# A long convolution woven into a feed-forward kernel: one pool for the kernel factors of all channel groups, earlier spectra, stores on another queue, another hand-out

## The chip, the cores and the metric

The kernel runs on one core of one Trainium2 chip. The time is what the device reports for one execution, in microseconds. The core has a matrix engine (PE, with its weight loads shown apart as PEld), a vector engine (DVE), a scalar engine (ACT), a general engine (POOL) and a sync engine (SP). SP, POOL and ACT can each start transfers between the chip's memory and the core; the profile names a started transfer by the queue of its engine (SPq, POOLq).

## The reference

The layer has two halves. A long causal convolution comes first, and a feed-forward part with ReLU after it; both are modulated by six vectors made from the condition c.

```
mod = silu(c) @ w_mod                      # sa, ca, ga, sb, cb, gb
h   = layernorm(x) * (1 + ca) + sa
K   = 2 * Re( sum_n C[d,n] * exp(A[d,n]*dt[d]*l) )     # l = 0..2047
x   = x + ga * ( causal_conv(h, K) + D_skip * h )      # by FFT in the reference
h   = layernorm(x) * (1 + cb) + sb
x   = x + gb * ( relu(h @ w1) @ w2 )
```

x is 2048 tokens by D = 576 channels, N = 128 states, w1 is 576 x 4608 and w2 is 4608 x 576, all in float32.

## The kernel before

**Tiling.** The 2048 tokens are cut into four blocks of 512. The convolution is done block by block in a transformed domain: the kernel K of each of four distances and the input of each block are transformed (function `transform` and the butterflies), their products are summed over the blocks (`product`), and the sum is transformed back and added to x (`inverse`). The transformed tiles, called spectra, hold 128 x 2304 numbers, 1152 KB each; they are stored in the chip's memory (Ud, Kd, Rd) and fetched again by POOL's queue (`load`).

**The kernel K** is not read but computed: for 12 channel groups of 48 channels each, `KGen.first` builds three factors, W1, W2 and Z, in the first 235 us and stores them (W1d, W2d, Zd). For distance 0 it multiplies them at once. For distances 1, 2 and 3 the function `KGen.rest` does it later: DVE turns W1 by Z once for each distance (`rot`, lines 459 to 465, four instructions), PE multiplies the result with W2 (`products`, line 490: 192 small matmuls per channel group, each with 16 columns per distance), ACT moves the products into a tile called ker (line 500), and after six channel groups `store` (line 431) writes ker to memory as kd, two transfers for each distance. `conv` reads it back as kt.

**The feed-forward part** runs through the four blocks, and in each through 36 groups g of 128 hidden units. To keep float32 accuracy each factor is split into a high and a low part and three products are made. `first(g)` has 14 matmuls into hps (line 1273); ACT makes the high part hh by ReLU (line 1278), DVE the low part hl (line 1279); `second(g)` has 14 matmuls of hh and hl with w2, into five accumulators (line 1299). PE's order is first(g+1), then second(g). In block 0 the weights come as float32 tiles r (SP, lines 1230 and 1234) and are split by ACT (1246, 1256) and DVE (1249, 1259, 1260); the low parts are stored (L1d, L2d) and read back in the later blocks, where DVE has no splits to do.

**What sets the order.** The convolution of block s+1 is a generator that is woven into the feed-forward part of block s. `step(g)` runs four times per group and takes pieces from the generator until a budget is reached: `rate` is the work handed out per step, a piece of DVE work counts its estimated microseconds, a burst of matmuls counts 0.7, `room` bounds the DVE work of the last four steps, and a piece that yields -1 ends the step. At the end of a block what is left of the generator is taken all at once. In block 0 the generator does `rest` for channel groups 0 to 5 and all three distances, then `rest` for 6 to 11 and distance 1 alone, each from a pool of its own, then conv(1). Block 1 adds block 0's result to x and writes it out (`finish(0)`), does `rest` for 6 to 11 and distances 2 and 3, then conv(2). Block 2 does finish(1) and conv(3). Within the limits of its program a scheduler moves instructions on each engine, so an instruction may stand earlier than the generator asked for.

**Buffers around the change.** In `rest`, W0 (the loaded W1), Z and W2 have two buffers each and are loaded together, one channel group ahead; W1r, the turned factor, has two; ker has one. The spectra share six buffers, and the products' half tiles T two. The x tile of block 1 comes from the pool `xb`, which is opened after `rest`. conv(1)'s normalised tile h2 has four buffers of its own, the tile xf two.

Of the kernel before, what the change touches and what calls it, by code (L numbers as in the profile page):

```python
# [49 lines left out]
class KGen:  # L50
# [384 lines left out]
    def rest(self, psum, hs, blocks):  # L435

# [3 lines left out]
        na = 16 * len(blocks)  # L440
        with ExitStack() as ctx:
            pt = k.pool(ctx, f"kr{hs[0]}{blocks[0]}", side="right")

            def load(h):
                W2 = pt.tile([P, 2, 32, H], F32, tag="W2", bufs=2, name=f"W2r_{h}")
                W0 = pt.tile([P, 16, 2, H], F32, tag="W0", bufs=2, name=f"W0_{h}")
                Z = pt.tile([P, 2, 2, H], F32, tag="Z", bufs=2, name=f"Zr_{h}")
                d = nc.gpsimd.dma_start
                d(out=W0.rearrange("p a r c -> p (a r c)"), in_=k.W1d[h])
                d(out=Z.rearrange("p i r c -> p (i r c)"), in_=k.Zd[h])  # L450
                d(out=W2.rearrange("p r b c -> p (r b c)"), in_=k.W2d[h])
                return W2, W0, Z

# [13 lines left out]

            def rots(W1, W0, Z):
# [12 lines left out]
            def products(h, W1, W2):  # L481
                if h % 6 == 0:
                    ke[0] = pt.tile([P, na, 72], F32, tag="ke", bufs=1, name=f"ker_{h}")
# [20 lines left out]
                if h % 6 == 5:  # L504
                    yield -1
                    for i, s in enumerate(blocks):
                        self.store(
                            s, h // 6, ke[0][:, 16 * i : 16 * i + 16].rearrange("p a q -> p (a q)"),
                            nc.gpsimd,
                        )  # L510

            nxt = load(hs[0])
# [21 lines left out]
class Body:  # L534
# [198 lines left out]
    def main(self, ctx, kg, hooks):  # L733
# [10 lines left out]
        def block0():  # L744
            yield from kg.rest(self.cps, range(0, 6), (1, 2, 3))
            yield from kg.rest(self.cps, range(6, 12), (1,))
            self.xp.append(self.pool(ctx, "xb"))
            self.x2p.append(self.xp[1])
            pool(1)
            yield from self.conv(1)  # L750

        def block1():
            yield from self.finish(0)
            yield -1
            self.cvs.close()
            yield from kg.rest(self.cps, range(6, 12), (2, 3))
            pool(2)
            yield from self.conv(2)
# [6 lines left out]
        with ExitStack() as c:  # L765
# [4 lines left out]
            self.nps = 4  # L770
# [13 lines left out]
        self.nps = 1  # L784
# [116 lines left out]
    def conv(self, s):  # L901
# [25 lines left out]
        yield -1  # L927
# [44 lines left out]
        def product(p, Y):  # L972
            def pair(t):
                Ka = Ks[p] if t == 0 else self.load(self.Kd[s - t][p], "Ka")
                Ua = Us[p] if (t == s and Us[p] is not None) else self.load(self.Ud[t][p], "Ua")
                return Ka, Ua
# [3 lines left out]
            yield -1  # L980
# [53 lines left out]
        Us, Ks, Vs = [], [], []  # L1034
# [20 lines left out]
        else:  # L1055
# [6 lines left out]
            ZK = self.spec("Z")  # L1062
            yield from both(spec_U(1, Z1), mm_K(1, ZK))
# [13 lines left out]
        else:  # L1077
            yield from both(spec_K(1, ZK), after(3, inverse(0, Vs[0])))
# [3 lines left out]
        yield -1  # L1082
        yield -1
# [15 lines left out]
        h2 = [self.cvl.tile([P, D + 64], F32, tag="h2", bufs=4, name="h2") for _ in range(4)]  # L1099
# [7 lines left out]
        for kk in (4, 0, 1, 2, 3):  # L1107
# [3 lines left out]
            xf = self.cvl.tile([P, 512], F32, tag="xf", bufs=2, name="xf")  # L1111
# [109 lines left out]
    def ffn(self, gens):  # L1221
# [87 lines left out]
        def step(g):  # L1309
# [5 lines left out]
            room = (9.0, 7.0, 7.0, 7.0)[g // NF] - sum(recent[-3:])  # L1315
            recent.append(0.0)
            while done[0] < target and v < min(room, 2.7) and pe < 2:
                w = next(gen, 0)
                if gen.gi_frame is None or w == -1:
                    return  # L1320
                if w is None:
                    pe += 1
                    done[0] += 0.7
                else:
                    v += w
                    recent[-1] = v
                    done[0] += w
# [85 lines left out]
    def rate(self, b):  # L1413
        return (2.12, 1.8, 1.4, 0.5)[b]
# [82 lines left out]
```

## Time and profile before

| what | value |
|---|---|
| median of 3 runs | 1408.16 us (1401.38 to 1409.32) |
| the profiled execution | 1404.99 us; its span, first to last instruction, 1403.2 us |
| mean granted PE clock | 0.936 of full speed |
| busy in the span | PE 1258.5, DVE 889.9, ACT 497.4, POOL 179.2 us |
| moved | 348.21 MB, 247 GB/s over the span |

The profile's page gives busy time per engine, the chain of work that ended last, and the costliest groups of instructions by line of the code. A view by windows gives each engine's busy time, the granted PE clock and the share of time that the transfer engines were busy, for a stretch of the span. A timeline gives single rows: start, duration, engine, line, operation, tile written and tiles read, and in brackets the idle time ahead with what ended it.

Marks for block 0: the first low part hl of group 0 starts at 237.71 us, that of group 13 at 354.73, 18 at 390.13, 23 at 461.58, 28 at 514.28, 35 at 591.01, the first two groups of block 1 at 616.27 and 618.34, and the next at 631.87. The four blocks thus take some 380 us from the first mark to the seventh, and then 771.33 us from 631.87 to the end.

### The profile page before, as it was taken

What the parts mean: (1) busy time and instruction counts of PE and PEld (TensorE: products, weight loads), DVE (VectorE), ACT (ScalarE), POOL (GpSimd) and SP (SyncE); (2) the same over time, 40 slices, a digit from 0 to 9 for tenths busy, and PEclk for the clock granted to TensorE, in tenths of its full rate; (3) what the DMA queues carried; (4) which work ended last, traced back from release to release, by engine and by line L of the source; (5) the groups of instructions that cost most, each with busy time, mean ns of one, the idle gap of its engine ahead of it and who ended that gap; (6) DMA issues with size and microseconds to landing.
All of it is one profiled execution on the core that took longest, in us unless ns stands there. A gap on an engine that the chain in (4) does not pass through costs nothing.

```text
span 1403.2 us, 26027 instructions
## 1 busy us (share of the span) xinstructions
PE 1258.5 (90%) x10720; PEld 994.5 (71%) x10720; DVE 889.9 (63%) x1324; ACT 497.4 (35%) x863; POOL 179.2 (13%) x277
## 2 busy tenths in 40 slices
PE   4565677899988997789999999999999999999997
PEld 2354555678866775567777787777887878888886
DVE  5989967999565778749825779563899332010102
ACT  4778323222211430252224322633332353232321
POOL 0677520000110100011010110000000000000000
PEclk9667786999999998889999999999999999999999
DMA  8658875767796776649777988584989657666661
GB/s 258 244 210 306 319 242 188 243 223 248 285 366 244 266 253 229 240 175 399 277 243 259 332 301 321 160 279 147 396 307 342 195 160 222 197 197 198 198 189 68
DMA packets 120843, 348.21 MB, mean 248 GB/s; under 512 B 23948, under 2 KB 24244, under 8 KB 109716
## 3 DMA queue, kind: packets, MB, share of 16 engines
q1 hardware_dynamic: 102260, 222.09, 47.4%
q0 software_dynamic: 17952, 123.08, 23.2%
q8 instruction: 84, 1.38, 0.4%
q10 hardware_dynamic: 512, 1.38, 0.3%
q14 instruction: 35, 0.29, 0.1%
HBM read 262.73 MB, written 83.76 MB: 247 GB/s over the span
## 4 chain that ended last, share of the span: by engine, by line
PE 62%; DVE 20%; DMA 9%; issue 4%; ACT 2%; POOL 1%; SPq 0%; ACTq 0%; POOLq 0%; DVEq 0%
PE acc L1299 24%; PE hps L1273 24%; PE kps L490 5%; PE ps_f L815 4%; DMA r<-in_w_dram 3%; DMA Ua<-Ud 3%; DVE T L998 3%; DVE Y L1000 3%; PE kps L71 2%; PE ph L71 2%; DMA Ud<-U 1%; DMA Zr<-Zd 1%; DVE hl L1279 1%; DVE Y L994 1%; DVE T L62 1%
## 5 line engine op out<-in xcount | busy, mean ns | idle before, releaser
L1273 PE MATMUL hps<-xh,w 128*128 128x512 f32 x1152 | 395.9, 403 | 0.7 <-issue 0.7
L1299 PE MATMUL acc<-w,hh 128*128 128x512 f32 x1152 | 368.2, 402 | 2.8 <-ACT hh L1278 2.8
L1279 DVE SCALAR_TENSOR_TENSOR hl<-hps,hh 128x512 fp32r<-128x512 f32 x144 | 99.2, 689 | 328.4 <-ACT hh L1278 328.1
L1299 PEld LDWEIGHTS acc<-w,hh 128*128 128x128 f32 x1152 | 217.0, 190 | 50.7 <-ACT hh L1278 3.6
L1273 PEld LDWEIGHTS hps<-xh,w 128*128 128x128 f32 x1152 | 219.0, 191 | 47.3
L1299 PE MATMUL acc<-w,hl 128*128 128x512 f32 x576 | 227.3, 406 | 20.4 <-DVE hl L1279 20.3
L1273 PE MATMUL hps<-xl,w 128*128 128x512 f32 x576 | 230.5, 401 | 0.9 <-DVE xl L47 0.9
L1278 ACT ACTIVATE hh<-hps 128x512 fp32r<-128x512 f32 x144 | 86.0, 597 | 317.9 <-PE hps L1273 317.9
L1256 ACT ACTIVATE w<-r 128x576 fp32r<-128x576 f32 x144 | 98.8, 686 | 279.8 <-PE acc L1299 226.0
L1299 PEld LDWEIGHTS acc<-w,hl 128*128 128x128 f32 x576 | 109.1, 191 | 48.3 <-DVE hl L1279 25.3
L1273 PEld LDWEIGHTS hps<-xl,w 128*128 128x128 f32 x576 | 110.0, 191 | 26.9 <-DVE xl L47 2.3
L1246 ACT ACTIVATE w<-r 128x640 fp32r<-128x640 f32 x144 | 105.4, 732 | 44.6 <-DMA r<-in_w_dram 44.2
L1273 PE MATMUL hps<-xs,w 128*128 128x512 f32 x288 | 100.9, 421 | 2.0 <-DVE xs L47 1.8
L490 PEld LDWEIGHTS kps<-W1r,W2r 128*32 128x32 f32 x3456 | 67.5, 146 | 35.6 <-issue 24.6
L490 PE MATMUL kps<-W1r,W2r 128*32 128x48 f32 (+2 forms) x3456 | 76.9, 238 | 11.9 <-issue 7.5
L71 PE MATMUL kps<-W,W 128*32 128x16 f32 x2304 | 44.8, 217 | 40.1 <-POOL W L68 29.0
L1000 DVE TENSOR_TENSOR Y<-Y,T 128x1152 f32<-128x1152 f32 x60 | 79.4, 1350 | 0.0
L71 PEld LDWEIGHTS kps<-W,W 128*32 128x32 f32 x2304 | 40.3, 150 | 51.1 <-POOL W L68 30.9
L816 ACT ACTIVATE Z<-ps_f 128x288 f32<-128x288 f32 x120 | 49.0, 409 | 70.7 <-PE ps_f L815 69.2
L1411 POOL DMA_DIRECT2D out_dram<-x x16 | 8.7, 546 | 458.3 <-DVE x L1403 455.9
L1273 PEld LDWEIGHTS hps<-xs,w 128*128 128x128 f32 x288 | 55.7, 196 | 15.1 <-ACT xh L47 2.1
L1299 PE MATMUL acc<-hh,w 128*128 128x512 f32 x144 | 57.9, 402 | 1.0 <-DVE w L1259 1.0
(234 smaller groups left out, 1593.5 us busy)
## 6 DMA issues: line engine op xcount, KB each, us to landing
r<-in_w_dram SPq DMA_DIRECT2D x144, 320.0 KB, 4.5
r<-in_w_dram SPq DMA_DIRECT2D x144, 288.0 KB, 3.2
w<-L1d SPq DMA_DIRECT2D x108, 320.0 KB, 2.7
w<-L2d SPq DMA_DIRECT2D x108, 288.0 KB
W2r<-W2d POOLq DMA_DIRECT2D x18, 1536.0 KB, 9.1
W2d<-W SPq DMA_DIRECT2D x12, 1536.0 KB, 8.6
Ua<-Ud POOLq DMA_DIRECT2D x15, 1152.0 KB, 9.6
W<-W1d POOLq DMA_DIRECT2D x18, 768.0 KB, 9.8
```

Source lines behind the costliest of these rows:

```text
L71: self.tc.keep_in_program_order(self.nc.tensor.matmul(*args, **kw))
L490: nc.tensor.matmul(ps[32 * dd : 32 * dd + 32, q, :], W2[:, r, :, ch], W1[:, :, r, ch], start=(r == 0), stop=(r == 1),)
L815: nc.tensor.matmul(o, fc[:, n2, c, :], src(n2), start=True, stop=True)
L816: ev = nc.scalar.activation(Z[:, n2, c], ps[:, :PC], AF.Copy)
L998: v(T, k, u, op=ALU.mult)
L1000: v(y, y, T, op=op or ALU.add)
L1246: nc.scalar.activation(w[:, 0], r, AF.Copy)
L1256: nc.scalar.activation(w[:, 0:D], r, AF.Copy)
L1273: nc.tensor.matmul(ps, a, x, start=(i == 0), stop=(i == 13))
L1278: nc.scalar.activation(hh, ps, AF.Relu)
L1279: nc.vector.scalar_tensor_tensor(hl, ps, 0.0, hh, op0=ALU.max, op1=ALU.subtract)
L1299: nc.tensor.matmul(acc[i], a, x, start=(f == 0 and seen[i] == 1), stop=(f == NF - 1 and seen[i] == (3 if i < 4 else 2)),)
```

## The change

- `rest` is called once for block 0. A plan says which distances each channel group takes: 0 to 5 all three, 6 to 11 the first. W0 and Z have three buffers and are loaded two channel groups ahead; W2 keeps two buffers and is loaded one ahead. Three one-distance groups share one tile W1r of 48 columns. ker has the full width throughout and one buffer.
- The kd stores are started by SP and no longer by POOL.
- The x tile of block 1 gets a pool of its own, opened before `rest`.
- Spectra have seven buffers instead of six, T three instead of two (in the first convolution still six and two). conv(1) to conv(3) take h2 and xf out of the spectra's buffers, xf four of them.
- The first input spectrum of each product is asked for before the butterflies that precede the product.
- The places that ended a step (`yield -1`) ahead of the transforms, ahead of each product and after the last `back` are gone for conv(1) to conv(3).
- In block 0 a burst of matmuls counts 0.35 instead of 0.7, room is 7.5 instead of 9.0, the rate 2.15 instead of 2.12.

```diff
-    def rest(self, psum, hs, blocks):
+    def rest(self, psum, plan):
         ...
-            def load(h):
-                W2 = pt.tile([P, 2, 32, H], F32, tag="W2", bufs=2, name=f"W2r_{h}")
-                W0 = pt.tile([P, 16, 2, H], F32, tag="W0", bufs=2, name=f"W0_{h}")
-                Z = pt.tile([P, 2, 2, H], F32, tag="Z", bufs=2, name=f"Zr_{h}")
+            def load0(h):
+                W0 = pt.tile([P, 16, 2, H], F32, tag="W0", bufs=3, name=f"W0_{h}")
+                Z = pt.tile([P, 2, 2, H], F32, tag="Z", bufs=3, name=f"Zr_{h}")
                 d(out=W0.rearrange("p a r c -> p (a r c)"), in_=k.W1d[h])
                 d(out=Z.rearrange("p i r c -> p (i r c)"), in_=k.Zd[h])
+                return W0, Z
+
+            def load2(h):
+                W2 = pt.tile([P, 2, 32, H], F32, tag="W2", bufs=2, name=f"W2r_{h}")
                 d(out=W2.rearrange("p r b c -> p (r b c)"), in_=k.W2d[h])
-                return W2, W0, Z
+                return W2
         ...
-                    ke[0] = pt.tile([P, na, 72], F32, tag="ke", bufs=1, name=f"ker_{h}")
+                    ke[0] = pt.tile([P, most, 72], F32, tag="ke", bufs=1, name=f"ker_{h}")[:, :na]
         ...
                         self.store(
                             s, h // 6, ke[0][:, 16 * i : 16 * i + 16].rearrange("p a q -> p (a q)"),
-                            nc.gpsimd,
+                            nc.sync,
                         )
         ...
+            nxt = [load0(hs[0])]
+            W2 = load2(hs[0])
+            nxt.append(load0(hs[1]))
             yield -1
             prev = iter(())
-            for h in hs:
-                W2, W0, Z = nxt
-                W1 = pt.tile([P, na, 2, H], F32, tag="W1", bufs=2, name=f"W1r_{h}")
-                yield from spread(rots(W1, W0, Z), prev, len(blocks))
-                if h + 1 in hs:
-                    nxt = load(h + 1)
+            for i, h in enumerate(hs):
+                W0, Z = nxt.pop(0)
+                if i + 2 < len(hs):
+                    nxt.append(load0(hs[i + 2]))
+                na = 16 * len(plan[h])
+                if used + na > most:
+                    all1 = pt.tile([P, most, 2, H], F32, tag="W1", bufs=2, name=f"W1r_{h}")
+                    used = 0
+                W1 = all1[:, used : used + na]
+                used += na
+                yield from spread(rots(h, W1, W0, Z), prev, len(plan[h]))
                 prev = products(h, W1, W2)
+                if i + 1 < len(hs):
+                    W2 = load2(hs[i + 1])
             yield from prev
         ...
         def block0():
-            yield from kg.rest(self.cps, range(0, 6), (1, 2, 3))
-            yield from kg.rest(self.cps, range(6, 12), (1,))
+            self.x2p.append(self.pool(ctx, "x2b"))
+            yield from kg.rest(
+                self.cps, {h: (1, 2, 3) if h < 6 else (1,) for h in range(NH)}
+            )
             self.xp.append(self.pool(ctx, "xb"))
-            self.x2p.append(self.xp[1])
         ...
-        return self.cv.tile([P, 4, 2, PC], F32, tag="S", bufs=6, name=name)
+        return self.cv.tile([P, 4, 2, PC], F32, tag="S", bufs=self.ns, name=name)
         ...
-        return self.cvl.tile([P, 4, PC], F32, tag="T", bufs=2, name=name)
+        return self.cvl.tile([P, 4, PC], F32, tag="T", bufs=self.ns - 4, name=name)
         ...
-                Ua = Us[p] if (t == s and Us[p] is not None) else self.load(self.Ud[t][p], "Ua")
+                Ua = first.pop(p) if p in first else Us[p] if (t == s and Us[p] is not None) else self.load(self.Ud[t][p], "Ua")
         ...
-            yield -1
+            if not s:
+                yield -1
         ...
             ZK = self.spec("Z")
+            first[0] = self.load(self.Ud[0][0], "Ua")
             yield from both(spec_U(1, Z1), mm_K(1, ZK))
         ...
         yield from back(1, Y)
-        yield -1
-        yield -1
         ...
-            room = (9.0, 7.0, 7.0, 7.0)[g // NF] - sum(recent[-3:])
+            room = (7.5, 7.0, 7.0, 7.0)[g // NF] - sum(recent[-3:])
         ...
-                    done[0] += 0.7
+                    done[0] += (0.35, 0.7, 0.7, 0.7)[g // NF]
         ...
-        return (2.12, 1.8, 1.4, 0.5)[b]
+        return (2.15, 1.8, 1.4, 0.5)[b]
```

The new lines push the later code down by some 20 lines: line 1279 (hl) before is line 1300 after, 1299 (acc) is 1320, 500 (ker) is 507.

Three places show what the change does to the order of the instructions. The rows give line, operation, tile written and tiles read with their numbers, and the shape.

**DVE at the end of block 0.** x_1 is the x tile of block 1, x_0 that of block 0; oT and t are block 0's result on its way into x_0 (`finish(0)`); xs and xl are the low parts of conv(1)'s result, which the first matmuls of block 1 read. Before, the last low part hl of block 0 is followed by 28 instructions until the two first hl of block 1; the last of these rows:

```order
L863 BN_STATS st_6298<-x_1_5282 128x6
L872 BN_AGGR mv<-st_6296 128x2
L872 BN_AGGR mv<-st_6297 128x2
L872 BN_AGGR mv<-st_6298 128x2
L1407 TENSOR_TENSOR oT<-oT,m_gb 128x512
L876 RECIPROCAL mv<-mv 128x1 x3
L877 SCALAR_TENSOR_TENSOR mv<-mv 128x1 x3
L1409 TENSOR_TENSOR x_0_280<-x_0_280,oT 128x512
L1407 TENSOR_TENSOR oT<-oT,m_gb 128x512 x2
L1409 TENSOR_TENSOR x_0_280<-x_0_280,oT 128x512 x2
L1119 TENSOR_TENSOR xs_6264<-xf,xs_6264 64x512
L1121 TENSOR_TENSOR xl_6263<-xf,xh_6262 128x512 x4
```

After, the last hl of block 0 is the second hl row here:

```order
L1280 TENSOR_TENSOR w_6352<-r_6231,w_6352 128x64
L1281 TENSOR_TENSOR w_6352<-r_6231,w_6352 128x512
L1300 SCALAR_TENSOR_TENSOR hl<-hps,hh 128x512
L1140 TENSOR_TENSOR xs_6148<-xf,xs_6148 64x512
L1300 SCALAR_TENSOR_TENSOR hl<-hps,hh 128x512
L1142 TENSOR_TENSOR xl_6147<-xf,xh_6146 128x512 x4
L1300 SCALAR_TENSOR_TENSOR hl<-hps,hh 128x512
L1428 TENSOR_TENSOR oT<-oT,m_gb 128x512
L1430 TENSOR_TENSOR x_0_280<-x_0_280,oT 128x512
L1428 TENSOR_TENSOR oT<-oT,m_gb 128x512
L1422 TENSOR_TENSOR t_6472<-ps_o_6467,m_gb 128x256
L1430 TENSOR_TENSOR x_0_280<-x_0_280,oT 128x512
```

The statistics of x_1 and conv(1)'s last inverse stand several groups earlier, the low parts xs and xl stand around block 0's last hl, and block 0's result comes after the first hl of block 1.

**ACT where ker passes from the first six channel groups to the last six.** ker with 48 columns is that of groups 0 to 5, ker with 16 columns that of 6 to 11; w is a split weight, r the loaded one. Before:

```order
L500 ACTIVATE ker_3101<-kps 128x48x6
L1278 ACTIVATE hh<-hps 128x512
L1246 ACTIVATE w_4475<-r_4443 128x640
L1256 ACTIVATE w_4678<-r_4445 128x576
L1278 ACTIVATE hh<-hps 128x512
L1246 ACTIVATE w_4684<-r_4627 128x640
L1256 ACTIVATE w_4845<-r_4629 128x576
L1278 ACTIVATE hh<-hps 128x512
L1246 ACTIVATE w_4851<-r_4785 128x640
L1256 ACTIVATE w_5003<-r_4787 128x576
L1278 ACTIVATE hh<-hps 128x512
```

After:

```order
L1277 ACTIVATE w_4514<-r_4267 128x576
L1267 ACTIVATE w_4322<-r_4265 128x640
L507 ACTIVATE ker_3119<-kps 128x48x6
L1299 ACTIVATE hh<-hps 128x512 x2
L507 ACTIVATE ker_4337<-kps 128x16x6
L1267 ACTIVATE w_4520<-r_4455 128x640
L507 ACTIVATE ker_4337<-kps 128x16x6
L1277 ACTIVATE w_4698<-r_4457 128x576
L507 ACTIVATE ker_4337<-kps 128x16x6
L1267 ACTIVATE w_4704<-r_4647 128x640
L507 ACTIVATE ker_4337<-kps 128x16x6
L1277 ACTIVATE w_4877<-r_4649 128x576
```

Before, four groups' hh lie between the last wide ker and the first narrow one (two more rows of w stand ahead of it); after, one group's pair of hh does, and the narrow ones follow each other with one w between.

**SP at the same place.** r is a loaded weight tile, L1d and L2d the stored low parts, kd the stored products. Before, with the kd stores on POOL:

```order
L1350 DMA L1d_141<-w_3994 128x640
L1234 DMA r_4316<-in_w_dram 128x576
L1230 DMA r_4314<-in_w_dram 128x640
L1350 DMA L2d_177<-w_4168 128x576
L1350 DMA L1d_142<-w_4071 128x640
```

After:

```order
L1371 DMA L1d_141<-w_4036 128x640
L431 DMA kd_0_59<-ker_3119 64x1152 x2
L431 DMA kd_0_61<-ker_3119 64x1152 x2
L431 DMA kd_0_63<-ker_3119 64x1152 x2
L1251 DMA r_4455<-in_w_dram 128x640
L1255 DMA r_4457<-in_w_dram 128x576
L1371 DMA L2d_177<-w_4316 128x576
```

The six stores stand in SP's order ahead of the next two weight loads. By the same listings the last turn of the factors (`rot`) stands in group 17 of block 0, before it stood in group 22; five and a half channel groups of products stand in groups 16 to 18, about two in each (before 1.2 in each of the groups 18 to 22); and the forward transforms of conv(1) stand in groups 20 to 24 (before 25 to 28). On DVE the eight statistics of the unchanged x_1 stand in the first 235 us, among the last instructions of conv(0); on POOL the load of x_1 stands after the copy of the condition (line 701 before), ahead of all of `rest`.

More of the change, by code (lines that the diff above doesn't have):

```diff
@@ L433, in store @@
             )
-    def rest(self, psum, hs, blocks):
+    def rest(self, psum, plan):
         nc, k = self.nc, self.k
         v = nc.vector.tensor_tensor
-        na = 16 * len(blocks)
+        hs = list(plan)
         with ExitStack() as ctx:
-            pt = k.pool(ctx, f"kr{hs[0]}{blocks[0]}", side="right")
-            def load(h):
-                W2 = pt.tile([P, 2, 32, H], F32, tag="W2", bufs=2, name=f"W2r_{h}")
-                W0 = pt.tile([P, 16, 2, H], F32, tag="W0", bufs=2, name=f"W0_{h}")
-                Z = pt.tile([P, 2, 2, H], F32, tag="Z", bufs=2, name=f"Zr_{h}")
-                d = nc.gpsimd.dma_start
+            pt = k.pool(ctx, f"kr{len(hs)}", side="right")
+            most = used = 16 * max(len(b) for b in plan.values())
+            d = nc.gpsimd.dma_start
+            def load0(h):
+                W0 = pt.tile([P, 16, 2, H], F32, tag="W0", bufs=3, name=f"W0_{h}")
+                Z = pt.tile([P, 2, 2, H], F32, tag="Z", bufs=3, name=f"Zr_{h}")
                 d(out=W0.rearrange("p a r c -> p (a r c)"), in_=k.W1d[h])
                 d(out=Z.rearrange("p i r c -> p (i r c)"), in_=k.Zd[h])
+                return W0, Z
+            def load2(h):
+                W2 = pt.tile([P, 2, 32, H], F32, tag="W2", bufs=2, name=f"W2r_{h}")
                 d(out=W2.rearrange("p r b c -> p (r b c)"), in_=k.W2d[h])
-                return W2, W0, Z
+                return W2
             def rot(out, X, Z, i):
@@ L466, in rot, with rots @@
                 yield 0.95
-            def rots(W1, W0, Z):
+            def rots(h, W1, W0, Z):
+                blocks = plan[h]
                 a = [W1[:, 16 * i : 16 * i + 16] for i in range(len(blocks))]
@@ L481, in products @@
             def products(h, W1, W2):
+                blocks = plan[h]
+                na = 16 * len(blocks)
                 if h % 6 == 0:
-                    ke[0] = pt.tile([P, na, 72], F32, tag="ke", bufs=1, name=f"ker_{h}")
+                    ke[0] = pt.tile([P, most, 72], F32, tag="ke", bufs=1, name=f"ker_{h}")[:, :na]
                 for half in range(2):
@@ L755, in block1 @@
             self.cvs.close()
-            yield from kg.rest(self.cps, range(6, 12), (2, 3))
+            yield from kg.rest(self.cps, {h: (2, 3) for h in range(6, NH)})
             pool(2)
@@ L769, in main @@
             self.cvl = self.pool(c, "cvl", side="right")
-            self.nps = 4
+            self.nps, self.ns = 4, 6
             mods, ffn = self.mod_late(), self.ffn(gens)
@@ L783, in main @@
             self.vec = nc.vector
-        self.nps = 1
+        self.nps, self.ns = 1, 7
         self.cps = self.pool(ctx, "cps", space=PSUM)
@@ L1032, in back @@
             Vs.append(V)
-        Us, Ks, Vs = [], [], []
+        Us, Ks, Vs, first = [], [], [], {}
         ZU = self.spec("Z") if s == 0 else None
@@ L1077, in conv @@
         else:
+            first[1] = self.load(self.Ud[0][1], "Ua")
             yield from both(spec_K(1, ZK), after(3, inverse(0, Vs[0])))
@@ L1081, in conv @@
         yield from back(1, Y)
-        yield -1
-        yield -1
         xh = xp.tile([P, 4, 512], F32R, tag="xh", bufs=1, name=f"xh_{s}")
@@ L1098, in conv @@
         yield 2.0
-        h2 = [self.cvl.tile([P, D + 64], F32, tag="h2", bufs=4, name="h2") for _ in range(4)]
+        flat = lambda name: self.spec(name).rearrange("p a b c -> p (a b c)")
+        h2 = [flat("h2")[:, : 2 * (D + 64)].rearrange("p (n d) -> p n d", n=2) for _ in range(2)]
+        h2 = [h2[n2 // 2][:, n2 % 2] for n2 in range(4)]
+        xfs = [flat("xf")[:, : 4 * 512].rearrange("p (k t) -> p k t", k=4)]
+        xfs = [xfs[0][:, k] for k in range(4)]
         for n2 in range(4):
@@ L1110, in conv @@
                 nc.tensor.transpose(ps[:, n2], h2[n2][:, kk * P : (kk + 1) * P], self.ident)
-            xf = self.cvl.tile([P, 512], F32, tag="xf", bufs=2, name="xf")
+            xf = xfs[kk % 4]
             ps = ps.rearrange("p a b -> p (a b)")
```

1 line of the change is left out of this document (removed).

## The prediction

> **What bounds the kernel now.** I read the page's busy times first, then the windows cut at the marks of block 0, then the idle times on PE's timeline, and last the chain of waits for what lies behind them.
>
> ```profile
> PE 1258.5 (90%) x10720; PEld 994.5 (71%) x10720; DVE 889.9 (63%) x1324; ACT 497.4 (35%) x863; POOL 179.2 (13%) x277
> ```
>
> PE is busy 90% of the span, so a gain must come from the stages where it is not, or runs at a lower clock. The windows (time, then busy time of PE, PEld, DVE, ACT, POOL, then granted PE clock, transfer share, GB/s):
>
> ```profile
> 237.71:354.73 117.02, 113.27 (x1321) 89.23 (x1320) 114.52 (x117) 28.15 (x48) 7.58 (x15) 0.97 0.72 249
> 354.73:390.13 35.40, 35.40 (x325) 28.99 (x325) 16.98 (x27) 10.29 (x17) 7.43 (x14) 1.00 0.83 304
> 390.13:461.58 71.45, 60.73 (x1294) 47.93 (x1293) 42.55 (x56) 12.65 (x28) 7.72 (x14) 0.93 0.81 296
> 461.58:514.28 52.70, 52.70 (x219) 38.38 (x218) 39.46 (x71) 23.59 (x53) 5.29 (x9) 1.00 0.81 287
> 514.28:591.01 76.73, 58.81 (x221) 44.99 (x220) 66.58 (x88) 13.68 (x22) 3.18 (x6) 0.88 0.62 227
> 591.01:618.34 27.33, 20.95 (x81) 15.10 (x82) 15.56 (x41) 17.45 (x32) 2.20 (x5) 0.77 0.20 64
> 631.87:890.00 258.13, 252.94 (x2117) 198.69 (x2118) 190.15 (x243) 79.51 (x150) 21.65 (x37) 0.99 0.82 296
> 890.00:1150.00 260.00, 259.02 (x1141) 208.53 (x1140) 168.12 (x236) 102.60 (x183) 12.37 (x22) 1.00 0.74 255
> 1150.00:1403.00 253.00, 245.30 (x1091) 203.24 (x1089) 37.68 (x58) 72.49 (x115) 4.32 (x8) 0.99 0.59 182
> ```
>
> From 631.87 on PE is busy 98% at a clock of 0.99 to 1.00: nothing to win there. Block 0 loses. What PE would need there comes from four prices in the chain and the timeline:
>
> ```profile
> 464.10 3.17 PE hps L1273 x14
> 467.27 3.17 PE acc L1299 x14
> 323.97 2.25 PE kps L490 x95
> 471.87 0.55 PE ps_f L815 x2
> ```
>
> A group is 2 x 3.17 = 6.35 us. A product of 48 columns is 2.25/95 = 0.0237 us, 192 of them 4.55 us per channel group; one of 16 columns is 0.0173 us (the 96 in 1.66 us below), 3.32 us. A pair of forward transforms is 0.56 us.
>
> - 237.71 to 390.13: 18 groups (114.3) and six wide channel groups (27.3) need 141.6; it took 152.4. Lost 10.8. DVE was busy 114.52 of the first 117.02 us: DVE bounds that.
> - 390.13 to 461.58: 5 groups (31.7) and six narrow channel groups (19.9) need 51.6 of 71.45. Lost 19.8.
> - 461.58 to 514.28: 5 groups and 32 pairs (17.9) need 49.6 of 52.7. Lost 3.1.
> - 514.28 to 618.34: 9 groups (57.1) and, estimated at full clock, some 11 us of small matmuls need 68.5 of 104.06. Lost 35.5.
>
> Together 69 us out of 380.6. The rows behind the second and the fourth, PE's timeline and the chain:
>
> ```profile
> 399.96 1.66 PE L490 MATMUL kps<-W1r,W2r 128*32 128x16 f32 x96 [4.41 <-ACT ker L500]
> 531.58 2.07 PE L1299 MATMUL acc<-w,hl 128*128 128x512 f32 x4 [6.09 <-DVE hl L1279]
> 543.89 1.19 PE L1299 MATMUL acc<-w,hl 128*128 128x512 f32 x4 [2.92 <-DVE hl L1279]
> 573.81 0.80 PE L1299 MATMUL acc<-w,hl 128*128 128x512 f32 x1 [5.48 <-DVE hl L1279]
> 381.59 17.39 DMA r<-in_w_dram
> 550.79 14.85 DMA r<-in_w_dram
> ```
>
> The first wait names ker on ACT, but ACT itself stood for r; a weight tile took 17.39 us to land just then. The next three are PE waiting for hl, because DVE had products of spectra queued ahead of it; after such a wait the matmuls run at about half rate for a while (four in 2.07 us, against 0.227 us each in the chain's 14). And 591 to 618 is the end of block 0: the generator is taken all at once and two groups need 27.33 us, at a clock of 0.77.
>
> **The change, part by part.** The prices on the other engines, from the groups of lines in the window 390.13 to 461.58, the timelines of POOL and DVE, and the transfers' issues (KB each, median us to landing):
>
> ```profile
> L459 DVE TENSOR_TENSOR T<-W,Zr 128x1536 f32<-128x1536 f32 x5 | 8.8, 1751 | 0.0
> L461 DVE TENSOR_TENSOR W1r<-W,Zr 128x1536 f32<-128x1536 f32 x5 | 8.8, 1751 | 0.0
> L463 DVE TENSOR_TENSOR W1r<-W1r,T 128x768 f32<-128x768 f32 x6 | 5.7, 953 | 0.0
> L465 DVE TENSOR_TENSOR W1r<-W1r,T 128x768 f32<-128x768 f32 x6 | 5.7, 952 | 0.0
> L1260 DVE TENSOR_TENSOR w<-r,w 128x512 fp32r<-128x512 f32 x6 | 4.1, 684 | 0.0
> L863 DVE BATCH_NORM_STATS2 st<-x 128x6 f32<-128x288 f32 x8 | 3.0, 444 | 0.0
> 369.19 3.17 POOL L431 DMA_DIRECT2D kd<-ker  x6 [36.51 <-ACT ker L500]
> 375.73 0.53 POOL L451 DMA_DIRECT2D W2r<-W2d  x1 [2.30 <-DMA kd<-ker]
> 628.53 1.76 DVE L459 TENSOR_TENSOR T<-W,Zr 128x1536 f32<-128x1536 f32 x1 [9.49 <-DMA Zr<-Zd]
> r<-in_w_dram SPq DMA_DIRECT2D x144, 320.0 KB, 4.5
> W2r<-W2d POOLq DMA_DIRECT2D x18, 1536.0 KB, 9.1
> kd<-ke SPq DMA_DIRECT2D x4, 288.0 KB, 2.4
> kd<-ker POOLq DMA_DIRECT2D x12, 288.0 KB, 6.0
> ```
>
> *Turning, groups 0 to 17.* The even hand-out moves turns, it removes none. One turn is 1.75 + 1.75 + 0.95 + 0.95 = 5.4 us by these rows, about 5.1 as the starts follow each other, 15.2 for three distances. In the changed order one wide channel group stands in two feed-forward groups (before, some two and a half). With splits and hl that makes DVE some 19.4 us per two groups, where PE needs 12.7 + 4.55 = 17.3. Adding up the first 16 groups of the changed order, DVE has about 146 us and PE 126. PE can run some 8.5 us ahead before a late hl stops it (second(g-1), first(g+1) and part of second(g)), so 11 us are lost, as now. The next part of the chain merely starts earlier: no gain here, a range of 8 to 14.
>
> *The narrow products, groups 16 to 18.* Now 5.5 channel groups stand in three feed-forward groups. PE needs 19.0 + 18.3 = 37.3 us. Their W2 is 5.5 x 1536 KB, beside weights, the two halves of the factors ahead, and six kd stores of 288 KB; I estimate 17.7 MB over about 50 us.
>
> ```profile
> 381.00:407.00 26.00, 21.59 (x263) 17.36 (x262) 15.40 (x18) 5.07 (x10) 2.66 (x5) 0.87 1.00 381
> ```
>
> That window shows what the transfer engines give when they are full: 381 GB/s at a share of 1.00, so 17.7 MB are 46 us, just under PE's need. Two waits are new. ker has one buffer, and the first narrow ker (the row after the pair of hh on ACT) waits until six stores have landed; behind it on ACT wait the next splits, and PE waits for both. By the kd rows that is 2.4 to 6.5 us (6.0 landing, or 369.19 to 375.73 in the two POOL rows); I take 5. And on SP the next r stands behind those stores: between its usual 4.5 and the 17.39 seen, so 0 to 13 us late; I take 8. With W2's buffers freed only by PE I add 5. Sum 18, against 19.8 now; bounds 8 and 30.
>
> [...]
>
> *Spectra, groups 19 to 37.* Transforms start five groups earlier, and the products, butterflies and inverse of conv(1) spread over groups 19 to 33, with seven spectra buffers and the first Ua loaded before it is needed. The most DVE work in one group falls to 10.95 us (by adding the durations; 16.6 before); with the 8.5 us of lead no hl is late, so the three waits above (14.5 us, and their half-rate tails) go. xs and xl stand around the last hl of block 0, and finish(0) goes behind the first hl of block 1: the last window's loss, 8.8 us (27.33 less 12.7 for two groups and some 5.8 of small matmuls), shrinks to some 4. What stays: an r behind large spectra (6 of the present 10.4 beyond the usual landing), 4 us for the hand-out's unevenness. Sum 14 instead of 35.5; bounds 4 and 25. The 3.1 of the stage between become 1.5.
>
> *Before and after.* x_1's load and eight statistics (444 ns each) move ahead of block 0. Three of the statistics stand before the last normalised tile of conv(0), 1.3 us on the path; the others lie in DVE's waits there. The load competes with the last factors. I take +2, bounds 0 and 4. At the start of block 1 the first Zr is issued behind four stores of x_0 as now, with less before it to hide them: +1.5, bounds 0 and 3. The rest of blocks 1 to 3 is bound by PE: 0, give or take 3.
>
> *Sum:* A 0, B 18 - 19.8 = -1.8, between -1.6, C 14 - 35.5 = -21.5, edges +3.5: -21.4 from the profiled execution's 1404.99 us, so 1383.6. The median of the runs is 3.2 us above that execution; I leave half of that in and say **1385 us**.
>
> **The rivals.**
>
> *Bound by the transfers.* Block 0's transfer share is 0.6 to 0.8 already, and the change packs what was spread over five groups into three. If B comes to its 28 and r is late again in C (20), the sum is +8.2 - 1.6 - 15.5 + 3.5 = -5.4: 1400. For it: the 17.39 us row, share 1.00. Against: loads two groups ahead take the factors out of that stretch.
>
> *The stores stop the splits (slower).* The kd stores now sit in SP's queue, and each must wait for ker on ACT. SP issues in order, so a store that waits holds every weight load behind it, and with one ker buffer ACT then waits for the store. This happens at three places: after the sixth and twelfth channel groups in block 0, and in block 1. At 17.39 - 4.5 = 12.9 us each that is 39 us. With B unchanged and C saved: 1404.99 - 21.5 - 1.6 + 3.5 + 38.7 = 1424. It decides from about 6 us per place on, where it eats the gain. For it: r has only two buffers per shape. Against: the two places in the order where r is asked for stand two groups ahead of its use, 12.7 us, and ker is done before SP comes to the store.
>
> *Moved, not removed.* DVE has as much work in block 0 as before, 295.65 us of 380.63:
>
> ```profile
> 237.71:618.34 380.63, 341.87 (x3453) 264.63 (x3452) 295.65 (x395) 105.82 (x198) 33.40 (x62) 0.94 0.70 250
> ```
>
> If the spectra's products come as late as now, because Ua or a spectra buffer is late, the hl waits return at other groups: C stays near 33, the time 1401 to 1409, say 1405. For it: DVE's 78%. Against: the products of the second half stand three to five groups earlier.
>
> **How the numbers follow.** Two versions of this kernel closer than 0.5% cannot be told apart, which is 1401.1 to 1415.2. The forecast has a chance of 0.56, the transfers 0.16 (half of them beyond 1401), the stores 0.14, no change 0.14. So faster 0.56 + 0.10 = 0.66 and a little for a smaller price of edges, 0.69; same 0.18; slower 0.13. The forecast's own range is its bounds added half-way, 1368 to 1398; to 8 in 10 it must take in the transfers and part of no change: 1367 to 1407.
>
> **What would show it.** The first hl of block 1 comes near 595 us instead of 616; no wait for hl above 2 us on PE after the forward transforms; the window of the narrow products at a transfer share of 0.95 or more; ACT idle before the first narrow ker for 2 to 7 us with a kd store as releaser; DVE idle before the first T of block 1 about as long as the 9.49 us above. Wrong would be: r landing later than 13 us at two places or more (stores), hl waits of 5 us in groups 28 to 36 (moved), or blocks 1 to 3 longer than 775 us, for which I have no mechanism.

## The result: 2.6% less time, and where it came from

| | before | after |
|---|---|---|
| median of six runs, us | 1407.88 (1401.38 to 1410.71) | 1369.17 (1367.4 to 1375.86) |
| ratio to before, 95% interval | | 0.9738 [0.9709, 0.9767] |
| the profiled execution, us | 1404.99 | 1371.99 |

The time lies in the range of the prediction, 16 us below its number. By its page the changed kernel has the same number of matmuls (10720) and the same DVE work (889.8 us, 889.9 before) in a shorter span; PE is busy for 1245.2 us, 1258.5 before.

Its span is cut at the low parts hl again. In the changed kernel number 0 starts at 243.30 us, 14 at 373.33, 15 at 386.03, 18 at 438.65, 20 at 456.17, 36 and 37 (the first two of block 1) at 585.85 and 592.49, 38 at 605.66. The windows, with the columns of the prediction's table:

```profile
243.30:373.33 130.03, 122.82 (x1539) 96.17 (x1538) 130.03 (x132) 30.67 (x53) 11.69 (x22) 0.99 0.68 233
373.33:386.03 12.70, 11.15 (x136) 9.13 (x135) 8.91 (x11) 0.60 (x1) 0.53 (x1) 1.00 1.01 406
386.03:438.65 52.62, 41.37 (x1126) 33.32 (x1127) 20.02 (x27) 9.90 (x24) 4.39 (x7) 0.84 0.74 263
456.17:523.20 67.03, 67.00 (x283) 51.53 (x282) 63.79 (x96) 25.22 (x50) 6.55 (x11) 1.00 0.83 283
523.20:592.49 69.29, 66.92 (x303) 53.30 (x302) 55.57 (x98) 30.43 (x54) 2.60 (x5) 1.00 0.73 252
605.66:1354.96 749.30, 746.90 (x4314) 605.21 (x4315) 391.13 (x527) 253.39 (x447) 33.06 (x57) 1.00 0.74 250
```

With the prediction's own prices, what PE needs and what was lost over it:

| stage of the changed kernel | PE needs | took | lost | forecast | lost before |
|---|---|---|---|---|---|
| turning, low part 0 to 14 | 88.9 + 27.3 = 116.2 | 130.03 | 13.8 | 11 | 10.8 |
| narrow products, 14 to 20 | 38.1 + 19.9 + 3.9 = 61.9 | 82.84 | 20.9 | 18 | 19.8 |
| spectra, 20 to 37 | 107.9 + 14.0 + 11 = 132.9 | 136.32 | 3.4 | 15.5 | 38.6 |

Seven of the 32 pairs of forward transforms (3.9 us) run ahead of low part 20 in the changed kernel, so they count there; the 11 us of small matmuls are the prediction's estimate. The whole gain of block 0 stands in the stage of the spectra: 35.2 us less are lost there, 4.1 more in the two stages ahead of it. In 456 to 592 us PE is busy nearly all the time at a clock of 1.00, where before the clock was 0.88 and 0.77 in the last two windows of block 0; on PE's timeline the one wait between low parts 20 and 36 that shows an engine as releaser is

```profile
552.12 0.50 PE L1320 MATMUL acc<-w,hl 128*128 128x512 f32 x1 [2.37 <-DVE hl L1300]
```

The account against the profiled execution: the first low part 5.6 us later, block 0 from low part 0 to 37 shorter by 31.4 (380.63 to 349.19; the 380 us named ahead of the prediction are block 0's alone), the step to low part 38 0.4 shorter (13.53 to 13.17), then to the last low part 7.6 shorter (756.90 to 749.30), behind it 0.8 longer: -33.0, which is 1371.99 - 1404.99. The row of before for the fourth part:

```profile
631.87:1388.77 756.90, 750.73 (x4314) 605.05 (x4315) 389.44 (x526) 254.00 (x446) 36.19 (x63) 1.00 0.73 248
```

The first low part is not a good measure of the change: in the twelve profiled variants below it starts between 236.8 and 246.0 us, at 245.7 in the one with the late x_1 and at 236.8 in one with the early x_1. Stretches inside the span are therefore compared from low part to low part. Each stretch is read from one profiled execution, and that execution can lie some us off its kernel's median: 5.0 above it without the early Ua, 10.5 above it with the late x_1 alone, 5.1 below it in the first run with the stores on POOL.

### The profile page after: what moved, and what is told of

Its sections match the earlier page's. It is cut to its first block, busy times and chain, and to the rows that moved or that the text cites. A ratio compares the mean times of both kernels' runs of the same rounds, so it can differ in the third digit from the quotient of the medians.

```text
span 1370.2 us, 26007 instructions
## 1 busy us (share of the span) xinstructions
PE 1245.2 (91%) x10720; PEld 989.9 (72%) x10720; DVE 889.8 (65%) x1324; ACT 495.4 (36%) x863; POOL 173.3 (13%) x265
## 4 chain that ended last, share of the span: by engine, by line
PE 72%; DVE 14%; DMA 6%; issue 4%; ACT 2%; POOL 1%; SPq 0%; ACTq 0%; POOLq 0%; DVEq 0%
PE acc L1320 29%; PE hps L1294 29%; PE ps_f L832 4%; PE kps L497 3%; DMA r<-in_w_dram 2%; PE ph L71 2%; PE kps L71 1%; PE ps_i L1038 1%; DVE W1r L465 1%; DVE T L62 1%; DVE T L463 1%; DMA Ua<-Ud 1%; DVE W L62 1%; DMA W2r<-W2d 1%; POOL cb L717 1%
## 5 line engine op out<-in xcount | busy, mean ns | idle before, releaser
L1294 PE MATMUL hps<-xh,w 128*128 128x512 f32 x1152 | 391.5, 400 | 0.0
L1320 PE MATMUL acc<-w,hl 128*128 128x512 f32 x576 | 223.4, 399 | 3.8 <-DVE hl L1300 3.8
L1320 PE MATMUL acc<-hl,w 128*128 128x512 f32 x144 | 57.3, 398 | 0.0
```

What stands on the lines that cost most here:

```text
L1294: nc.tensor.matmul(ps, a, x, start=(i == 0), stop=(i == 13))
L1320: nc.tensor.matmul(acc[i], a, x, start=(f == 0 and seen[i] == 1), stop=(f == NF - 1 and seen[i] == (3 if i < 4 else 2)),)
```

## The experiments

Each is the changed kernel with one edit, unless said otherwise. "Block 0" is low part 0 to 38 (394.2 us before, 362.4 after), "blocks 1 to 3" is 38 to the last (756.9 and 749.3).

**The hand-out undone.**

```diff
-            room = (7.5, 7.0, 7.0, 7.0)[g // NF] - sum(recent[-3:])
+            room = (9.0, 7.0, 7.0, 7.0)[g // NF] - sum(recent[-3:])
-                    done[0] += (0.35, 0.7, 0.7, 0.7)[g // NF]
+                    done[0] += 0.7
-        return (2.15, 1.8, 1.4, 0.5)[b]
+        return (2.12, 1.8, 1.4, 0.5)[b]
```

> The changed kernel with the hand-out of before in block 0 (a matmul burst counts 0.7, room 9.0, rate 2.12); all else as changed. Theory 'spread': the 34 us that the spectra's part of block 0 gained come from the convolution's DVE work standing earlier and evenly, which the hand-out sets; undone, low parts hl are late again and the end of block 0 is drained at once: the first low part of block 1 comes 12 to 25 us later than in the changed kernel (585.85 there), total 1381 to 1394 us. Rival 'buffers': seven spectra buffers and the earlier Ua did it; then block 0 stays within 4 us and the total within 1366 to 1374. Blocks 1 to 3 unchanged under both (their numbers are not touched).

Measured: 1369.77 us, ratio 0.9734 [0.9703, 0.9765]; block 0 361.7 us. Low part 18 comes after 169.9 us instead of 195.4 and low part 36 after 345.9 instead of 342.6: the work stands elsewhere, the time is the same. "Spread" failed as I had put it: with the rest of the change in place, the even hand-out is worth nothing. The first forward transform of conv(1) on PE starts 204.6 us after low part 0, against 204.7 in the changed kernel (232.8 before).

**Spectra undone** (six buffers, two T, no early Ua), and then **the early Ua alone** and **six buffers alone**.

```diff
-        self.nps, self.ns = 1, 7
+        self.nps, self.ns = 1, 6
-            first[0] = self.load(self.Ud[0][0], "Ua")
...
-            first[1] = self.load(self.Ud[0][1], "Ua")
```

> The changed kernel with six spectra buffers, two half tiles T and no early request of the first Ua in conv(1) to conv(3); hand-out and single pool as changed. 'Spread': block 0 loses 3 to 8 us of its gain, blocks 1 to 3 lose the 7.6 us they gained (from the third low part of block 1 to the end they take 749 us in the changed kernel, 757 before), total 1376 to 1385. 'Buffers': block 0 loses 20 us or more and the total is 1392 to 1402. If neither moves (within 3 us), the buffers do nothing and the 7.6 us come from the removed ends of a step.

> The changed kernel without the early request of the first Ua, with seven spectra buffers and three T kept: splits the 16 us that the spectra's undoing cost. If a late Ua is what makes low parts wait, nearly all of the 16 us show: 1381 to 1386, with a DVE wait for a Ua of 5 to 9 us ahead of the first product. If the number of buffers is what counts, 1368 to 1373.

> The changed kernel with six spectra buffers, the early Ua and three T kept. The early Ua alone cost nothing in blocks 1 to 3 when it was taken out (750.3 us from the third low part of block 1 to the last, against 749.3), six buffers, two T and no early Ua together cost 7.6. So the seventh buffer or T should carry the 7.6: 756 to 758 us there if it is the seventh buffer, 749 to 751 if it is T. In block 0 it stays within 4 us of 362.4 if the early Ua needs no more room than six buffers give, and is 8 to 18 us longer if the early request then waits for a buffer. Total 1375 to 1395 or 1366 to 1374.

The last of them keeps three T by an edit of its own, since the number of T follows that of the spectra's buffers.

| | median | ratio to before | block 0 | blocks 1 to 3 |
|---|---|---|---|---|
| changed kernel | 1369.17 | 0.9738 [0.9709, 0.9767] | 362.4 | 749.3 |
| spectra undone | 1385.53 | 0.9839 [0.981, 0.9868] | 372.0 | 756.9 |
| no early Ua | 1384.64 | 0.9826 [0.9798, 0.9854] | 380.3 | 750.3 |
| six buffers, early Ua, three T | 1378.84 | 0.9786 [0.9761, 0.9811] | 362.5 | 755.5 |

The kernel with the spectra undone came out between its two expectations in block 0 (9.6 us lost), and without the early Ua the total was as expected, but the wait for the Ua shorter (3.92 us below, where 5 to 9 were expected). The two parts divide cleanly when each is taken out alone. Without the early Ua the profiled execution is 18 us longer in block 0 and 1 in the later blocks; by the medians it is worth 15.5 in all. The seventh buffer is worth nothing in block 0 and 6.2 of the 7.6 us in blocks 1 to 3. Undone together they cost less in block 0 (9.6) than the Ua alone; the slow profiled execution without the Ua can be a part of that, and the rest is open. In the kernel without the early Ua the stretch from low part 20 to 37 shows it, with the same DVE work as the changed kernel (119.6 us; 119.4 there) and 16.9 us more time; behind it the row of DVE's timeline where the first product begins:

```profile
454.10:526.84 72.74, 70.78 (x300) 54.50 (x298) 63.86 (x96) 25.88 (x51) 5.99 (x10) 1.00 0.71 244
526.84:607.33 80.49, 69.33 (x287) 52.69 (x286) 55.74 (x98) 29.93 (x53) 3.12 (x6) 0.92 0.66 230
```

```profile
488.86 1.36 DVE L1015 TENSOR_TENSOR T<-K,Ua 128x1152 f32<-128x1152 f32 x1 [3.92 <-DMA Ua<-Ud]
```

DVE stands 3.92 us for the first Ua, against 0.89 at 478.78 in the changed kernel:

```profile
478.78 2.63 DVE L1015 TENSOR_TENSOR T<-K,Ua 128x1152 f32<-128x1152 f32 x2 [0.89 <-DMA Ua<-Ud]
```

Counted from low part 0 the first product starts 11 us later (246.9 us against 235.5) and the second one, whose Ua is asked for behind the spectra of K instead of ahead of them, 13 us later (298.8 against 285.5). The work is then pushed together, and PE stands for hl (PE's timeline of that kernel):

```profile
557.06 0.79 PE L1318 MATMUL acc<-w,hl 128*128 128x512 f32 x1 [4.75 <-DVE hl L1298]
```

That is a wait of the kind that the kernel before had three times (6.09, 2.92 and 5.48 us).

**Two pools, alone and with the old hand-out; and all three parts undone together.**

```diff
-            yield from kg.rest(
-                self.cps, {h: (1, 2, 3) if h < 6 else (1,) for h in range(NH)}
-            )
+            yield from kg.rest(self.cps, {h: (1, 2, 3) for h in range(6)})
+            yield from kg.rest(self.cps, {h: (1,) for h in range(6, NH)})
```

> The changed kernel with rest called twice in block 0 as before (groups 0 to 5 with three distances, then 6 to 11 with one, each from a pool of its own), loads two ahead within each call, stores on SP and hand-out as changed. If the single pool is what lets the factors of the narrow groups come early, the second call waits for its first W0 and W2 (9 to 10 us landing each): the narrow products end 8 to 14 us later and the total is 1376 to 1384. Rival: the turning stage is bound by DVE and the lost time is hidden by the 8.5 us of lead, total 1367 to 1373.

> Two calls of rest and the hand-out of before together, spectra as changed. Alone the two cost 12 and 0 us, and with the spectra undone too the whole gain of 38 us went. If single pool and hand-out stand in for each other, this kernel is 20 to 30 us above the changed one: 1389 to 1399. If the hand-out never matters, it is at 1379 to 1383, and the excess lies between pools and spectra.

> The changed kernel with three parts undone together: two calls of rest with a pool each, six spectra buffers (two T) and no early Ua, and the hand-out of before. What remains of the change: loads two ahead, kd stores on SP, the early x_1, shared W1r, h2 and xf in the spectra's buffers, fewer ends of a step. If the parts add up (12 us for two pools, 16 for the spectra, 0 for the hand-out, each measured alone), the total is 1394 to 1400 and the rest of the change is worth 8 to 14 us. Rival 'joint': the single pool and the hand-out give the same thing twice, so that undoing either alone costs little and both together more: 1402 to 1410, about the time of before, and the rest of the change is worth nothing.

| | median | ratio to before |
|---|---|---|
| two pools | 1380.86 | 0.9802 [0.9761, 0.9842] |
| two pools, old hand-out | 1387.06 | 0.9851 [0.9829, 0.9874] |
| two pools, old hand-out, spectra undone | 1410.35 | 1.0012 [0.9995, 1.003] |

With two pools POOL cannot start the narrow groups' first loads until the last wide product has run; POOL's and DVE's timelines:

```profile
365.52 0.53 POOL L449 DMA_DIRECT2D W<-W1d  x1 [34.01 <-PE kps L497]
```

```profile
385.98 0.23 DVE L1279 TENSOR_TENSOR w<-r,w 128x64 fp32r<-128x64 f32 x1 [11.07 <-ACT w L1276]
```

and ACT's timeline:

```profile
385.26 0.69 ACT L1276 ACTIVATE w<-r 128x576 fp32r<-128x576 f32 x1 [11.08 <-DMA r<-in_w_dram]
```

DVE stands there for a split of the weight r, not for the factors: the first W0 and Z landed 5.9 and 6.2 us after POOL asked for them, some 20 us before the first narrow turn at 392.75, which stands behind that split in DVE's order. The r was asked for behind the kd stores, in the same 6 us as POOL's eight loads, and took 14.70 us. So the wait that was expected, for the first W0 and W2, is not what the trace shows; in the changed kernel DVE turns factors through this passage and has no gap before 373.33 us. The last narrow ker then comes 213.5 us after low part 0 instead of 192.9 (8 to 14 us later were expected), and the first forward transform after 225.3 instead of 204.7 (231.5 with the old hand-out too).

The total with two pools lies where it was expected; with the old hand-out as well it lies between its two expectations. The hand-out, worth nothing with one pool, is worth some 6 us with two (1387.06 to 1380.86), which is not clear of the noise, as the intervals overlap a little. And the three together give back the time of before, as "joint" expected: what is left of the change (loads two ahead, stores on SP, the early x_1, fewer ends of a step) is worth nothing as a whole without them; its members were not all tried alone, and some may cancel. The sum of the three alone, 12 + 16 + 1, is 29 of the 41 us. So the parts stand in for each other: with one of them undone the others still save part of its time. My reading is that the one pool lets the convolution start early and the early Ua lets it go on.

**The late x_1, and with it a third W2 buffer in block 0.**

```diff
-            self.x2p.append(self.pool(ctx, "x2b"))
...
+            self.x2p.append(self.xp[1])
-                W2 = pt.tile([P, 2, 32, H], F32, tag="W2", bufs=2, name=f"W2r_{h}")
+                W2 = pt.tile([P, 2, 32, H], F32, tag="W2", bufs=3 if len(hs) == NH else 2, name=f"W2r_{h}")
```

> The changed kernel with a third W2 buffer in block 0; the space comes from opening x_1's pool after rest, as before the change, so that x_1's load and statistics go back into conv(1). Theory 'W2 chain': in the changed kernel the narrow products are bound by W2 loads that can start only when the products two channel groups earlier have freed a buffer (389.1, 400.6, 411.0, 417.7 us, each about 9 us to landing); with one more buffer the stretch from the last wide ker to the eighteenth low part, 386.0 to 438.7, shrinks by 7 to 13 us. Rival 'transfers': the stretch is bound by what the transfer engines can move or by late weights, and it stays within 3 us. Undoing the early x_1 gives 1 to 3 us before block 0 and costs 2 to 5 us at its end. Total by the first 1358 to 1366, by the second 1368 to 1374.

> The changed kernel with x_1's pool opened after rest, so that its load and eight statistics go back into conv(1): the control for the third W2 buffer. If that run's loss behind the narrow products (7 us between the twentieth low part and the third of block 1) came from the late x_1, it shows here too and the total is 1374 to 1380. If the narrow products' time was merely given back because later stages wait for something else, the total is 1367 to 1373 here as well.

Measured: 1370.46 (0.9731 [0.9699, 0.9763]) with the third buffer, 1370.01 (0.9741 [0.9698, 0.9785]) with the late x_1 alone. Low part 15 to 20 takes 64.3 and 63.8 us, against 70.1 in the changed kernel, so the third buffer adds nothing to the late x_1. Whether the 6 us are the late x_1's is not shown: three other kernels with the early x_1 and the stores on SP, those of the spectra's parts, take 66.4 to 70.5 there, and two executions of one kernel (below) differ by 5.0. Both give the 6 us back from low part 20 to 38 (156.7 and 161.8, against 149.5). "W2 chain" failed: a wait of W2 for a buffer does not bind the narrow products.

**The kd stores back on POOL**, measured twice.

```diff
-                            nc.sync,
+                            nc.gpsimd,
```

> The changed kernel with the kd stores back on POOL. My forecast put 13 us of the narrow products' loss on ker waiting for its stores and on the weights behind them on SP; on POOL the stores stand ahead of the factor loads instead. If the stores on SP cost what I took, this kernel is 4 to 10 us faster between low parts 15 and 20 (70.1 us in the changed kernel). If their queue matters little, that stretch and the total stay within 4 us, 1366 to 1374. If POOL's loads then come late, the total is 1375 to 1385.

> The changed kernel with the kd stores on POOL once more, in five rounds, since its four earlier runs lay between 1355.1 and 1369.7 us. If the 7 us between it and the changed kernel are real, the ratio to before is 0.964 to 0.970 with an interval that ends below 0.971 and block 0 (first low part to the third of block 1) is 352 to 357 us again against 362.4; if they were scatter, the ratio is 0.971 to 0.976.

Measured: 1361.99 us, ratio 0.967 [0.9618, 0.9722], and 1363.95, ratio 0.9688 [0.9667, 0.9708], against 0.9738 [0.9709, 0.9767] with the stores on SP. Low part 15 to 20 takes 59.2 and 64.2 us instead of 70.1, block 0 354.6 and 357.3 instead of 362.4, as expected, give or take 1 us. This kernel is faster than the one before and than the changed one: 5 us below the changed one by the second measurement, whose interval just clears that of the changed kernel. SP's timeline of the changed kernel, its chain of waits, and ACT's timeline show what the stores do:

```profile
370.29 4.15 SPq L431 DMA_DIRECT2D kd<-ker  x6
```

```profile
374.54 14.72 DMA r<-in_w_dram
```

```profile
386.75 0.26 ACT L507 ACTIVATE ker<-kps 128x96 f32<-128x96 f32 x1 [5.71 <-DMA kd<-ker]
389.29 0.74 ACT L1267 ACTIVATE w<-r 128x640 fp32r<-128x640 f32 x1 [2.28 <-DMA r<-in_w_dram]
```

SP starts six stores, and the weight r asked for right behind them takes 14.72 us to land; ACT waits 5.71 us for the stores and then for r. The stores are not shown to be all of r's delay: the transfer engines are full there (share 1.01 in 373 to 386 us), and POOL's loads of W0 and Z from the same 6 us took 11.3 to 14.2 us as well. On POOL the stores, started in 3.16 us, stand ahead of the next factor instead; my reading is that this delays the turning of the narrow groups and so thins out their products: DVE is busy for 8.46 us between low parts 14 and 16 of the first run, for 16.23 in the changed kernel. The runs do not separate these effects. SP bought no faster landing here: ACT's wait for the stores ends 12.9 us after SP started the last of them, and on POOL they took 11.1 to 13.6 us.

**Stores on POOL, the late x_1 and a third W2 buffer.**

> kd stores on POOL, a third W2 buffer in block 0, x_1's pool after rest. With the stores out of the way of the weights, the wait of a W2 load for a free buffer is what is left in the narrow products (three of 7.8, 4.9 and 11.2 us on POOL there). If that binds, the total is 3 to 8 us below the kernel with kd on POOL alone: 1352 to 1359. If it is given back later, as with kd on SP, the total is 1359 to 1364.

Measured: 1374.41, ratio 0.9761 [0.9736, 0.9786], 10 us slower than the stores on POOL alone; both expectations missed. From low part 20 to 38 it takes 164.1 us (157.7 and 160.0 with the stores on POOL alone); why the late x_1 and the third buffer cost time here and none with the stores on SP, the runs do not show. Low part 15 to 20 takes 66.6 us, and PE's products wait in it for no other engine. The groups of PE's products in that stretch, of this kernel, of the first run with the stores on POOL (15 to 20), and of the changed kernel (15 to 20):

```profile
L497 PE MATMUL kps<-W1r,W2r 128*32 128x16 f32 x1056 | 19.7, 214 | 9.2 <-issue 9.2
```

```profile
L497 PE MATMUL kps<-W1r,W2r 128*32 128x16 f32 x1056 | 19.3, 212 | 2.1 <-issue 2.1
L1320 PE MATMUL acc<-w,hh 128*128 128x512 f32 x37 | 11.8, 398 | 3.0 <-issue 3.0
```

```profile
L497 PE MATMUL kps<-W1r,W2r 128*32 128x16 f32 x1056 | 19.3, 213 | 12.8 <-issue 9.3 <-ACT ker L507 2.9 <-DMA W2r<-W2d 0.6
```

"issue" is time in which PE waited for nothing that the profile shows. It is 9.3 of the 12.8 us that PE stands still there in the changed kernel; the last section shows where these waits stand.

## Why the prediction was right, and where it was off

- **The sign and the place were right.** The gain lies where the prediction put it: where three waits for hl stood, one of 2.37 us does (the prediction allowed none above 2); the half-rate tails and the drained end of block 0 are gone (the twelve matmuls behind that wait start within 2.86 us, and the clock in the last two stretches of block 0 is 1.00).
- **The spectra's term was mis-sized.** It kept 15.5 us: 4 at the end of block 0, 6 for a late r, 4 for the hand-out's unevenness, and 1.5 ahead of them. Measured are 3.4. No r stands in that stretch's chain of waits; the one long transfer in it is a Ua of 13.42 us, which leads to the 2.37 us. (A slip of 0.4 us is in the prediction's need: 57.1 and 11 are 68.1, not 68.5.)
- **The number was near partly by luck.** The spectra came out 12.1 us better, blocks 1 to 3 7.6 and the start of block 1 1.9; the turning was 3.0 worse, the narrow products 2.9 and the first low part 3.6. Errors both ways left 11.6 us between forecast and profiled execution.
- **The narrow products' term was near in size and wrong in its make-up.** Taken were 18 us, measured 20.9. The waits that it named were there on their engines: ACT waited 5.71 us for the stores (5 taken), and r took 14.72 us, 10.2 over the 4.5 of before (8 taken; the changed kernel's own median is 7.7). But of these 13 us PE stood for 2.9, by the last row of the experiments. The third, 5 us for W2's buffers, was the wrong mechanism: W2's wait is 0.6 us, and a third buffer brings nothing. In their place stand 9.3 us of issue, and some 8 us of matmuls slower than the price, at a mean granted clock of 0.90 from low part 14 to 20. The transfer share of 0.95 that the prediction asked for is there for 12.7 us only (1.01), then it is 0.74: after those 12.7 us the transfers do not bind this stage, and as a cause for all of it that rival falls.
- **The turning** lost 13.8 where 11 was taken; DVE is busy 130.03 of 130.03 us, as the prediction had it.
- **The edges.** The start of the span moves more from profile to profile than the 2 us taken for the early x_1, so that term is neither shown nor refuted. The start of block 1 cost -0.4 instead of +1.5: DVE waits 9.14 us for the first Zr, as before (9.49).
- **Blocks 1 to 3** were taken as 0, give or take 3, because PE is busy 98% there. They gave 7.6: a busy share of 98% at full clock still left them room. Half of it was PE's idle time (6.2 us to 2.4), half its busy time (750.73 to 746.90). Six buffers alone lose 6.2 of it.
- **The rival of the stores** had the right sign and the wrong price: stores on SP cost 5 us in all, not 13 at each of three places, and by which of the effects above is not shown. That SP issues in order shows at the first place: it stood 9.4 us for ker, started the six stores from 370.29 us on, and the two weight loads behind them at 374.54 and 375.14. Its sign, an r later than 13 us, does not tell the cases apart: the kernel before shows it too (17.39 and 14.85 us).
- **The rival "moved, not removed"** named the right condition: with Ua late, the waits for hl do come back (the kernel without the early Ua), and 15 us with them.

## What to carry to other kernels

Count a stage's loss against what its engine needs at the prices of an undisturbed stretch, and count each kind of work in the stage where it runs; that shows which stage can gain. Ask for a large operand before the work that precedes its use, as soon as a buffer can take it: without two lines of that kind 15 of the 39 us are lost here. The parts of such a change stand in for each other, so undo them alone and together before one is called idle. When an engine's wait names another engine, follow that engine's own wait: here DVE's named ACT, and ACT's named a weight. Try a store on both queues: here the queue that feeds the next weights was the dearer one, by 5 us.

## What was not expected of the hardware

PE lost 9.3 us to issue in the stretch of 1056 small products of the changed kernel. With the stores on POOL the two rows above add up to 5.1 (6.7 in the second run), and to 9.2 with the third buffer and the late x_1. In 372 to 440 us the changed kernel's transfer queues also carried ten instruction packets, of 16384 bytes each:

```profile
q8 instruction: 10, 0.16, 1.0%
```

With all of PE's instruction records (weight loads, matmuls and those of its sequencer) counted from the start of the span, the four waits stand at:

| wait for issue, us | ends at, us | the instruction packet before it ended at, us | number of PE's record |
|---|---|---|---|
| 2.32 | 393.47 | 391.91 | 9411 |
| 2.75 | 399.67 | 398.22 | 9667 |
| 0.52 | 416.34 | 415.06 | 10435 |
| 3.71 | 428.29 | 426.94 | 10946 |

The numbers are 256, 768 and 511 apart, and each wait ends 1.3 to 1.6 us after such a packet. The same holds in the other traces: of 53 waits for issue above 0.4 us between low parts 0 and 37 of the fourteen profiles, 50 stand 194 or 195 records past a multiple of 256 and end 1.0 to 1.6 us after an instruction packet. (The other three, of 6.8 to 7.5 us, are in the kernels with two pools, at the first narrow product.) My reading of these distances is that PE stood for its next instructions, and that such a packet brought them; no view shows whose instructions a packet holds. No run varied this alone, so what the whole stretch would gain without these waits is not measured. Open is also why block 0 loses less with the spectra buffers and the Ua both undone than with the Ua alone.
